# Second mlp in two halves of its width, with blocks in pairs

## Chip, cores and metric

The kernel runs on one core of one Trainium2 chip. The metric is the device time of one execution in microseconds (us), as the median of several runs; less is better.

## The reference, cut to what matters

Three layers follow each other on 4 x 768 = 3072 tokens of 384 values: a linear attention with a decaying state (8 heads of 48), a soft mixture of experts (8 experts of 4 slots, width 1024), and a second mlp of width 2048. All is float32.

```python
def _attn_ref(r, k, v, w, u):
    for t in range(S):
        cur = np.einsum('bhd,bhe->bhde', u[None] * kt, vt)
        y[:, :, t] = np.einsum('bhd,bhde->bhe', rt, state + cur)
        state = w[None, :, :, None] * state + np.einsum('bhd,bhe->bhde', kt, vt)
def _moe_ref(x, phi, w1, w2):
    logits = x @ phi
    # d: softmax over the tokens, c: softmax over the 32 slots
    slot_input = d.T @ x
    for e in range(E):
        h = np.maximum(slot_input[e] @ w1[e], 0.0)
        slot_out[e] = h @ w2[e]
    return c @ slot_out
def _moe2_ref(x, w_in, w_out):
    h = x @ w_in
    g = np.maximum(0.01 * h, h)
    return g @ w_out
```

The inputs w_in and w_out of the second mlp come as float64 and have to be brought to float32 on the chip; all other inputs are float32.

## The kernel before, in words

One function, `chunked`, writes the work out by hand (its order on each engine is the order of the code). It has three parts.

*The attention* goes over 24 units `i`, one for each of 6 chunks of 128 tokens and 4 pairs of heads. Each unit loads its rows `rkb` and its tokens `tk` from HBM four units ahead; GpSimd scales and multiplies them (lines 300, 306, 309, 338), VectorE scales the other half (300), masks the scores (`copy_predicated`, 357), sums a diagonal (314) and adds to the state (410); TensorE computes scores, outputs and updates (349, 380, 387, 400). Every fourth unit adds a softmax over the slots (lines 457 to 509). Beside it the weights of the later parts are loaded: `WST` says at which unit the next tile is loaded by `load_weights`, first 8 tiles `wir` of w_in (128 x 768 values of 8 bytes, as pairs of integers), then the 16 tiles of w1. They lie in the pool `wp`, a ring of `NWT` = 16 buffers of 6 KiB per partition. The tiles of w_in are brought to float32 in half tiles, one in each of the units of `NARROW` (4 to 19): `narrow_a` on ScalarE into PSUM (`nra`, line 166), and `narrow_b`, `narrow_c` and `narrow_d` on VectorE (lines 170, 174, 180), whose result goes to `wi` in SBUF.

*The experts* are TensorE's: `hidden` (line 718) and `outer` (line 761), with the last rows of w2 (`load_rows`) and all eight tiles `wor` of w_out (`load_wout`) loaded meanwhile into buffers of the ring that come free.

*The second mlp* never forms the tokens' x. The 32 slots' outputs are multiplied with w_in once, G = slot_out x w_in (`pG`, line 849: 32 x 2048, in two halves of columns `x`, four column groups `j` of 512 side by side in the partitions). G is split in a rounded value and its rest (`gch`, `gcl`), and `spread` (lines 868, 869) brings each group back to a layout of 128 rows, `Gs`. Then 96 steps `n` follow, one for each of 6 blocks of 512 tokens and 16 tiles `f` of 128 columns of the width, block by block (`seq`, line 874). A step has a hidden matmul (`hid_a`: `h` in PSUM, line 893, and its scaling by 0.01 on ScalarE, line 897), the maximum on VectorE (`hid_b`, line 900, into `t`), a rounded copy on ScalarE (`hid_c`, line 903, `gh`) and the rest that the rounding lost (`hid_d`, line 907, `gl`; on GpSimd in the first 16 steps, on VectorE later). `product` (line 946) adds nine matmuls to the three output tiles of the block: gh x woh, gh x wol and gl x woh, where woh and wol are w_out rounded and its rest. The hidden matmul runs three steps ahead of its product, the cast and the rest two steps ahead:

```python
        if n + 2 < n_seq:
            hid_c(n + 2)
        if n + 3 < n_seq:
            hid_a(n + 3)
```

PSUM holds two tiles of `h` (pool `pH`) and two sets of three output tiles (pool `pP`): eight tiles of 128 x 512 together. Within the first 12 steps a chunk `p` of w_out is narrowed every second step: `conv_a` on ScalarE (line 806, the abs of the high word, into `wfa` in SBUF), `conv_b`, `conv_c`, `conv_d` on VectorE (again lines 170, 174, 180, whole tiles of 768 columns). `parts(f)` then makes woh on ScalarE (line 821) and wol on GpSimd (line 822), one tile f per step. At the end of a block `store` copies its three tiles to SBUF (line 953) and SP stores them; the last three tiles f of the last block are done output tile by output tile.

Of the kernel before, what the change touches and what calls it, by code (L numbers as in the profile page):

```python
# [115 lines left out]
def chunked(ctx, tc, rk, tok, wT, urep, phi, w1, w2, win, wout, outT, dbg=None, check=False):  # L116
# [655 lines left out]

    def load_rows(f):
        t = wp.tile([128, 4, DM], F32, name=f"w2_{f}", tag="wt")
        nc.sync.dma_start(t, w2[4:, :, f].rearrange("e p d -> p e d"))
        for g in range(4):
            w2_sb[FT * (4 + g) + f] = t[:, g]
# [64 lines left out]
    gch = ep.tile([128, 512], F32R, name="gch", tag="hs", bufs=2)  # L842
    gcl = ep.tile([128, 512], F32R, name="gcl", tag="hs", bufs=2)
    for x in range(2):
        k = slice(x * 256, x * 256 + 256)
        pG = pE.tile([128, 256], F32, name=f"pG{x}", tag="ph")
# [7 lines left out]
        nc.scalar.copy(gch[:, k], pG)
        nc.vector.tensor_tensor(gcl[:, k], pG, gch[:, k].bitcast(F32), op=ALU.subtract)
        if x == 0:
            parts(0)
            conv_b(1)
        else:
            conv_c(1)  # L860


    def spread(j, xs, pool, tag):
        pg = pool.tile([128, 2, 256], F32, name=f"pg{j}{xs[0]}", tag=tag)
        hi, lo = (sel[:, j, z : z + 4].rearrange("p a s -> p (a s)") for z in (1, 0))
        for n, x in enumerate(xs):
            k = slice(x * 256, x * 256 + 256)
            nc.tensor.matmul(pg[:, n], hi, gch[:, k], start=True, stop=False)
# [200 lines left out]
```

## Time and profile before

| what | us |
|---|---|
| median of 3 runs | 419.74 |
| lowest and highest run | 418.54, 421.74 |
| the profiled execution, whole | 415.55 |
| its span (first to last instruction) | 413.8 |
| TensorE busy in the span | 384.6 |
| VectorE busy | 291.5 |
| ScalarE busy | 236.7 |
| GpSimd busy | 153.1 |

The profile is of one execution, a little faster than the median. Times in its rows count from the start of the span. An engine's busy time is the time in which one of its instructions ran; what an engine waited for before an instruction stands behind the bar in the view by groups of lines, and in brackets in the timeline. A matmul of float32 operands shows as two instructions in the trace (48 for the 24 of `pG`). Numbers at the end of a line name in the view by stretch: TensorE's granted clock as a share of full speed, the share of time in which the DMA engines were busy, and GB/s.

### The profile page before, as it was taken

What the parts mean: (1) busy time and instruction counts of PE and PEld (TensorE: products, weight loads), DVE (VectorE), ACT (ScalarE), POOL (GpSimd) and SP (SyncE); (2) the same over time, 40 slices, a digit from 0 to 9 for tenths busy, and PEclk for the clock granted to TensorE, in tenths of its full rate; (3) what the DMA queues carried; (4) which work ended last, traced back from release to release, by engine and by line L of the source; (5) the groups of instructions that cost most, each with busy time, mean ns of one, the idle gap of its engine ahead of it and who ended that gap; (6) DMA issues with size and microseconds to landing.
All of it is one profiled execution on the core that took longest, in us unless ns stands there. A gap on an engine that the chain in (4) does not pass through costs nothing.

```text
span 413.8 us, 7910 instructions
## 1 busy us (share of the span) xinstructions
PE 384.6 (93%) x2929; PEld 289.6 (70%) x2929; DVE 291.5 (70%) x496; ACT 236.7 (57%) x544; POOL 153.1 (37%) x142
## 2 busy tenths in 40 slices
PE   5798998989999999988889999999999999999993
PEld 3477786868676444666568888888888888888882
DVE  6988999999994642898866666665656575665650
ACT  4577777777786402686665554645555555555440
POOL 4989997978770400299992000000000000000000
PEclk9979999999999999999999999999999999999998
DMA  7969999999999899910002000200200020001002
GB/s 257 408 246 389 410 399 408 397 408 389 407 360 326 267 358 389 417 54 0 1 2 77 0 2 0 76 2 1 78 0 0 2 77 0 2 36 40 2 0 84
DMA packets 20944, 70.06 MB, mean 169 GB/s; under 512 B 2225, under 2 KB 7073, under 8 KB 20769
## 3 DMA queue, kind: packets, MB, share of 16 engines
q1 hardware_dynamic: 20896, 69.47, 43.9%
q8 instruction: 25, 0.41, 0.4%
q14 instruction: 23, 0.18, 0.2%
HBM read 64.74 MB, written 4.72 MB: 168 GB/s over the span
## 4 chain that ended last, share of the span: by engine, by line
PE 60%; DVE 22%; ACT 5%; POOL 4%; issue 4%; DMA 2%; SPq 1%; DVEq 0%; ACTq 0%; POOLq 0%
PE o L946 43%; DVE base L357 5%; PE h L893 5%; ACT base L329 3%; PE po L761 3%; PE ph L718 3%; DVE wor L174 2%; DVE Sbd L410 2%; DVE rkb L300 2%; DVE Dg L314 2%; POOL gl L907 2%; DVE nra L174 2%; DMA rkb<-in_rk_dram 2%; PE A L349 1%; DVE wor L170 1%
## 5 line engine op out<-in xcount | busy, mean ns | idle before, releaser
L903 ACT CAST gh<-t 128x512 fp32r<-128x512 f32 x94 | 58.4, 621 | 70.6 <-DVE t L900 67.5
L907 DVE TENSOR_TENSOR gl<-t,gh 128x512 fp32r<-128x512 f32 x80 | 55.4, 692 | 58.7 <-ACT gh L903 56.9
L946 PE MATMUL o<-gl,woh 128*128 128x512 f32 x282 | 82.1, 396 | 0.7 <-POOL gl L907 0.7
L946 PE MATMUL o<-gh,wol 128*128 128x512 f32 x282 | 82.2, 396 | 0.0
L946 PE MATMUL o<-gh,woh 128*128 128x512 f32 x282 | 81.4, 393 | 0.0
L900 DVE TENSOR_TENSOR t<-t,h 128x512 f32<-128x512 f32 x96 | 65.7, 685 | 16.4 <-ACT t L897 16.0
L897 ACT ACTIVATE t<-h 128x512 f32<-128x512 f32 x96 | 57.3, 598 | 23.0 <-PE h L893 16.2
L329 ACT ACTIVATE base<-anti,Dg 128x128 f32<-128x128 f32 x184 | 56.3, 389 | 15.2 <-DVE Dg L314 15.0
L946 PEld LDWEIGHTS o<-gl,woh 128*128 128x128 f32 x282 | 52.9, 188 | 14.2 <-POOL gl L907 1.6
L946 PEld LDWEIGHTS o<-gh,wol 128*128 128x128 f32 x282 | 53.0, 188 | 12.7
L946 PEld LDWEIGHTS o<-gh,woh 128*128 128x128 f32 x282 | 52.9, 188 | 11.6
L893 PE MATMUL h<-cT,Gs 128*128 128x512 f32 x96 | 38.5, 405 | 5.7 <-DVE t L900 5.2
L300 POOL TENSOR_TENSOR rkb<-rkb,ET 112x512 f32<-112x512 f32 x24 | 31.9, 1328 | 11.4 <-DMA rkb<-in_rk_dram 11.4
L349 PE MATMUL A<-rkb 48*128 48x128 f32 x384 | 29.7, 297 | 6.5 <-DVE base L357 3.4
L357 DVE COPY_PREDICATED base<-mask,A 128x512 f32<-128x512 int32 x48 | 32.5, 727 | 2.1 <-PE A L349 1.1
L349 PEld LDWEIGHTS A<-rkb 48*128 48x128 f32 x384 | 25.2, 199 | 11.7 <-POOL tk L309 4.4
L822 POOL TENSOR_TENSOR wol<-wor,woh 128x384 fp32r<-128x384 f32 x16 | 22.1, 1385 | 28.8 <-PE pg L869 28.5
L893 PEld LDWEIGHTS h<-cT,Gs 128*128 128x128 f32 x96 | 18.0, 189 | 14.0 <-DVE t L900 9.5
L387 PE MATMUL y<-base,tk 128*48 128x128 f32 (+1 forms) x376 | 26.4, 284 | 0.0
L306 POOL TENSOR_TENSOR tk<-tk,u_sb 128x384 f32<-128x384 f32 x23 | 24.6, 1068 | 2.2 <-DMA tk<-in_tok_dram 1.1
L309 POOL TENSOR_TENSOR tk<-tk 128x384 f32<-128x384 f32 x23 | 24.1, 1048 | 1.8
L387 PEld LDWEIGHTS y<-base,tk 128*48 128x48 f32 (+1 forms) x376 | 20.2, 127 | 3.9 <-issue 1.0
(181 smaller groups left out, 489.8 us busy)
## 6 DMA issues: line engine op xcount, KB each, us to landing
w<-in_w_dram SPq DMA_DIRECT2D x24, 768.0 KB, 8.6
tk<-in_tok_dram SPq DMA_DIRECT2D x23, 576.0 KB, 7.1
rkb<-in_rk_dram SPq DMA_DIRECT2D x24, 512.0 KB, 7.3
wir<-in_win_dram SPq DMA_DIRECT2D x8, 768.0 KB, 9.0
wor<-in_wout_dram SPq DMA_DIRECT2D x8, 768.0 KB, 14.5
out_dram<-obs SPq DMA_DIRECT2D x18, 256.0 KB, 2.3
w2t<-in_w_dram SPq DMA_DIRECT2D x4, 576.0 KB, 5.9
rkb<-in_w_dram SPq DMA_DIRECT2D x4, 384.0 KB, 7.0
```

The source lines that it names most:

```text
L300: (nc.vector if x else eng).tensor_tensor(t, t, e, op=ALU.mult)
L306: eng.tensor_tensor(rr, rr, u_sb[:, hp : hp + 1, :].broadcast_to([128, B, 2 * D]), op=ALU.mult)
L329: nc.scalar.activation(base[i][:, h, b, :], anti, AF.Copy, scale=Dg[i][:, h * B + b : h * B + b + 1])
L349: nc.tensor.matmul(a[:, h, b, :], rk_t[i][p0 : p0 + D, 1, b, :], rk_t[i][p0 : p0 + D, 0, b, :], start=True, stop=True,)
L357: nc.vector.copy_predicated(base[i][:, :, 2 * j : 2 * j + 2, :], mask.unsqueeze(1).unsqueeze(1).broadcast_to([128, 2, 2, C]), a[:, :, 2 * ...
L387: nc.tensor.matmul(y[64 * h : 64 * h + n, b, :], v[:, b, D * h : D * h + n], base[i][:, h, b, :], start=c == 0, stop=True, skip_group_chec ...
L893: nc.tensor.matmul(h, Gs[f // 8][:, f % 8 * 128 : f % 8 * 128 + 128], cT[blk // 3][:, blk % 3 * TB : blk % 3 * TB + TB], start=True, stop= ...
L897: nc.scalar.mul(tt[n], h, 0.01)
L900: nc.vector.tensor_tensor(tt[n], tt[n], hps[n], op=ALU.max)
L903: nc.scalar.copy(gh[n], tt[n])
L907: eng.tensor_tensor(gl[n], tt[n], gh[n].bitcast(F32), op=ALU.subtract)
L946: nc.tensor.matmul(os[m], w[j][:, k, m * 128 : (m + 1) * 128], g[n], start=f == 0 and w is woh and g is gh, stop=f == NFT - 1 and g is gl,)
```

## The change

The width of the second mlp is done in two halves of eight tiles f, and within a half the six blocks go in three pairs: for each tile f the two blocks of the pair follow each other, so that a tile of w_out serves two steps in a row (`seq`). Only the last two blocks of the second half go one after the other. After the first half of a block its three output tiles are copied to SBUF (`sums`, six tiles of the ring); after the second half `store` adds the PSUM tiles to them on VectorE and stores the sum.

What only the second half needs is done within the first. Four of the eight tiles of w_in (0 to 3, columns of the first half) are loaded and narrowed in the attention, in eight units instead of sixteen; the other four are loaded after the experts and narrowed whole at steps 14, 18, 22 and 26 (in SBUF, as w_out is). Their buffers then take the tiles 4 to 7 of w_out (`again`), which are narrowed at steps 34, 38, 42 and 46. A table `jobs` says what is done in which step. The second half of G is computed at step 30 in a PSUM tile of `h`, and spread at steps 32 and 33. GpSimd makes `gl` for odd steps of the first half, VectorE for all others. `WST` has 22 tiles instead of 24: four of w_in, sixteen of w1, two rows of w2; the ring has 18 buffers instead of 16. `conv_b` of chunk 1 stands in the code ahead of the steps and again at step 0.

The core of the diff (with new functions in full; left out are the renamed layout of w_in, tiles that change their pool, and the debugging output):

```diff
-NWT = 16
+NWT = 18
...
-WST = [2, 3, 4, 5, 5, 6, 7, 8, 9, 9, 10, 11, 12, 13, 13, 14, 15, 16, 17, 17, 18, 19, 20, 21]
-NARROW = list(range(4, 20))
+WST = [2, 3, 4, 5, 6, 7, 8, 8, 9, 10, 11, 12, 12, 13, 14, 15, 16, 17, 19, 20, 21, 22]
+NARROW = [5, 7, 9, 11, 12, 14, 16, 18]
 WCH = 8
+WH = WCH // 2
...
+    for j in range(WH, WCH):
+        wirs[j] = wp.tile([128, WCW, 2], I32, name=f"wir{j}", tag="wt")
+        load_wide(win[j], wirs[j])
...
+    def g_mm(x, pool, tag):
+        pG = pGs[x] = pool.tile([128, 256], F32, name=f"pG{x}", tag=tag)
         for kt in range(KT):
             for j in range(4):
                 nc.tensor.matmul(
                     pG[32 * j : 32 * j + 32, :], soT[:, kt, :],
...
+                    wi[:, j, kt * 256 : kt * 256 + 256], start=kt == 0, stop=kt == KT - 1,
...
+    def g_parts(x, pool, tag):
...
+        nc.scalar.copy(gch[x], pGs[x])
+        nc.vector.tensor_tensor(gcl[x], pGs[x], gch[x].bitcast(F32), op=ALU.subtract)
...
+    g_mm(0, pE, "ph")
+    g_parts(0, ep, "hs")
+    parts(0)
+    conv_b(1)
...
-    seq = [(blk, f) for blk in range(NTOK // TB) for f in range(NFT)]
+    seq = [
+        (blk, f) for x in range(2) for two in range(0, NB, 2)
+        for f in range(NFT // 2 * x, NFT // 2 * (x + 1)) for blk in (two, two + 1)
+    ]
+
+    seq[-NFT:] = sorted(seq[-NFT:])
...
-        eng = nc.gpsimd if 0 < n < NFT else nc.vector
+        eng = nc.gpsimd if 0 < n < n_seq // 2 and n % 2 else nc.vector
...
     hid_c(1)
-    conv_d(1)
+    parts(1)
     hid_d(1)
     late[1](nc.scalar.copy)
-    late[2](nc.vector.tensor_copy)
-    late[3](nc.scalar.copy)
+    conv_a(1)
...
     def store(blk, m, o):
-        ob = obs[blk % 2][:, m, :]
-        (nc.scalar.copy if m % 2 else nc.vector.tensor_copy)(ob, o)
-        nc.sync.dma_start(outT[m * 128 : (m + 1) * 128, blk * TB : (blk + 1) * TB], ob)
+        t = sums[blk][:, m, :]
+        nc.vector.tensor_tensor(t, t, o, op=ALU.add)
+        nc.sync.dma_start(outT[m * 128 : (m + 1) * 128, blk * TB : (blk + 1) * TB], t)
...
+    def convert(p, n):
+        if p > 1:
+            job(n - 2, conv_a, p)
+        job(n, conv_b, p)
+        job(n, conv_c, p)
+        job(n + 1, conv_d, p)
+        if p < WCH:
+            job(n + 2, parts, 2 * p)
+            job(n + 3, parts, 2 * p + 1)
+
+    for p in range(1, WH):
+        convert(p, 4 * (p - 1))
+    def again(p):
+        wor[p] = wirs[p]
+        load_wide(wout[p], wor[p])
+
+    for q in range(WH):
+        convert(WCH + q, 4 * q + 14)
+        job(4 * q + 18, again, WH + q)
+        convert(WH + q, 4 * q + 34)
+    late = {}
+    job(30, g_mm, 1, pH, "h")
+    job(31, g_parts, 1, gp, "g1")
+    for q in range(2):
+        job(32 + q, lambda q: late.update({q: spread(1, (2 * q, 2 * q + 1), pH, "h")}), q)
+        job(32 + q, lambda q: late[q](nc.scalar.copy), q)
...
+        for fn, a in jobs.get(n, ()):
+            fn(*a)
         if not last:
             product(n, range(KT), pout[blk])
+        if f == NFT // 2 - 1:
+            for m in range(KT):
+                (nc.vector.tensor_copy if m % 2 else nc.scalar.copy)(
+                    sums[blk][:, m, :], pout[blk][m]
+                )
```

Chunks `p` of 8 and above are the tiles of w_in: `raw(p)` is `wor[p]` below 8 and `wirs[p - 4]` from there, and `conv_d` of those writes `wi[:, p - 8]`.

What moves on the engines shows at three places. First VectorE in the attention: one unit and the beginning of the next, before:

```order
L300 TENSOR_TENSOR rkb_111<-rkb_111,ETp 112x512
L357 COPY_PREDICATED base_998<-mask,A_1041 128x2x256 x2
L314 TENSOR_REDUCE Dg_1069<-tk_871 128x4x2
L410 SCALAR_TENSOR_TENSOR Sbd<-Sbd,W_138,U_1081 48x4x48 x2
L170 TENSOR_SCALAR wir_557<-wir_557 128x384
L174 SCALAR_TENSOR_TENSOR nra_1032<-nra_1032,wir_557 128x384
L180 SCALAR_TENSOR_TENSOR wi<-wir_557,nra_1032 128x384
L300 TENSOR_TENSOR rkb_112<-rkb_112,ETp 112x512
```

and after the change, at the unit with the same buffer `rkb_111`:

```order
L300 TENSOR_TENSOR rkb_111<-rkb_111,ETp 112x512
L357 COPY_PREDICATED base_981<-mask,A_1022 128x2x256 x2
L314 TENSOR_REDUCE Dg_1050<-tk_859 128x4x2
L410 SCALAR_TENSOR_TENSOR Sbd<-Sbd,W_138,U_1062 48x4x48 x2
L300 TENSOR_TENSOR rkb_112<-rkb_112,ETp 112x512
```

The three instructions of the narrowing are gone from this unit; the unit ahead of it keeps its own.

Second, VectorE at the start of the second mlp, before (the number behind `t`, `g`, `h` and `gl` is the step, that behind `wor` the chunk of w_out):

```order
L855 TENSOR_TENSOR gcl_2338<-pG0_2339,gch_2337 128x256
L170 TENSOR_SCALAR wor1_2165<-wor1_2165 128x768
L855 TENSOR_TENSOR gcl_2338<-pG1_2357,gch_2337 128x256
L174 SCALAR_TENSOR_TENSOR wor1_2165<-wfa_2277,wor1_2165 128x768
L900 TENSOR_TENSOR t0_2382<-t0_2382,h0_2381 128x512
L900 TENSOR_TENSOR t1_2387<-t1_2387,h1_2386 128x512
L907 TENSOR_TENSOR g0_2383<-t0_2382,g0_2383 128x512
L180 SCALAR_TENSOR_TENSOR wor1_2165<-wor1_2165 128x768
L871 CAST Gs1_2172<-pg20_2399 128x512
L900 TENSOR_TENSOR t2_2436<-t2_2436,h2_2435 128x512
L170 TENSOR_SCALAR wor2_2167<-wor2_2167 128x768
L174 SCALAR_TENSOR_TENSOR wor2_2167<-wfa_2277,wor2_2167 128x768
```

and after:

```order
L876 TENSOR_TENSOR gcl0_2311<-pG0_2297,gch0_2310 128x256
L170 TENSOR_SCALAR wor1_2071<-wor1_2071 128x768
L925 TENSOR_TENSOR t0_2322<-t0_2322,h0_2321 128x512
L925 TENSOR_TENSOR t1_2326<-t1_2326,h1_2325 128x512
L932 TENSOR_TENSOR g0_2125<-t0_2322,g0_2125 128x512
L925 TENSOR_TENSOR t2_2364<-t2_2364,h2_2363 128x512
L932 TENSOR_TENSOR gl2_2366<-t2_2364,gh2_2365 128x512
L925 TENSOR_TENSOR t3_2375<-t3_2375,h3_2374 128x512
L170 TENSOR_SCALAR wor1_2071<-wor1_2071 128x768
L174 SCALAR_TENSOR_TENSOR wor1_2071<-wfa_2223,wor1_2071 128x768
L925 TENSOR_TENSOR t4_2398<-t4_2398,h4_2397 128x512
L180 SCALAR_TENSOR_TENSOR wor1_2071<-wor1_2071 128x768
```

The maxima t0 to t3 now stand ahead of the second and third part of chunk 1's narrowing, `gl2` and `gl4` are VectorE's, and chunk 2 does not come in these rows any more.

Third, TensorE at G, before (`pG0` and `pG1` are the two halves of G, `pg` are spreads):

```order
L849 MATMUL pG0_2339<-wi_74,soT_2332 32x256 x12
L849 MATMUL pG1_2357<-wi_74,soT_2332 32x256 x12
L868 MATMUL pg00_2375<-gch_2337,sel_2054 128x256
L869 MATMUL pg00_2375<-gcl_2338,sel_2054 128x256
L893 MATMUL h0_2381<-cT0_2161,Gs0_2171 128x512
L893 MATMUL h1_2386<-cT0_2161,Gs0_2171 128x512
L868 MATMUL pg01_2391<-gch_2337,sel_2054 128x256
L869 MATMUL pg01_2391<-gcl_2338,sel_2054 128x256
```

and the second half of G after the change, at step 30 (`o2_0` to `o2_2` are the output tiles of block 2, `h33` and `h34` hidden matmuls of steps 33 and 34):

```order
L918 MATMUL h33_2971<-cT1_2122,Gs0_2123 128x512
L867 MATMUL pG1_2980<-wi_74,soT_2292 32x256 x12
L967 MATMUL o2_0_0_2697<-gh30_2918,woh0_2220 128x512
L967 MATMUL o2_1_0_2698<-gh30_2918,woh0_2220 128x512
L967 MATMUL o2_2_0_2699<-gh30_2918,woh0_2220 128x512
L967 MATMUL o2_0_0_2697<-gh30_2918,wol0_2222 128x512
L967 MATMUL o2_1_0_2698<-gh30_2918,wol0_2222 128x512
L967 MATMUL o2_2_0_2699<-gh30_2918,wol0_2222 128x512
L967 MATMUL o2_0_0_2697<-gl30_2919,woh0_2220 128x512
L967 MATMUL o2_1_0_2698<-gl30_2919,woh0_2220 128x512
L967 MATMUL o2_2_0_2699<-gl30_2919,woh0_2220 128x512
L918 MATMUL h34_3006<-cT1_2122,Gs0_2123 128x512
```

The twelve matmuls of `pG1` went from the wait before step 0 to between the hidden matmul of step 33 and the product of step 30.

## Rows read from the trace of the kernel before

**Rows 1.** view by stretch, four stages; columns are named in its first line

```profile
core 0: us, PE busy (x) PEld busy (x) DVE busy (x) ACT busy (x) POOL busy (x), PEclk, DMA share, GB/s
45.00:124.20 79.20, 73.89 (x1062) 59.56 (x1062) 75.82 (x155) 60.46 (x186) 66.17 (x63) 1.00 1.00 397
...
138.80:166.40 27.60, 27.33 (x270) 11.41 (x270) 12.01 (x28) 5.06 (x14) 4.40 (x10) 1.00 0.99 349
...
175.16:212.06 36.90, 30.98 (x122) 21.77 (x121) 32.85 (x33) 24.84 (x45) 35.37 (x23) 1.00 0.06 23
212.06:406.80 194.74, 194.71 (x837) 156.79 (x835) 117.69 (x174) 102.63 (x173) 7.58 (x7) 1.00 0.06 24
```

**Rows 2.** the chain that ended last, from the page, by line

```profile
PE o L946 43%; DVE base L357 5%; PE h L893 5%; ACT base L329 3%; PE po L761 3%; PE ph L718 3%; DVE wor L174 2%; DVE Sbd L410 2%; DVE rkb L300 2%; DVE Dg L314 2%; POOL gl L907 2%; DVE nra L174 2%; DMA rkb<-in_rk_dram 2%; PE A L349 1%; DVE wor L170 1%
```

**Rows 3.** groups of lines between 45 and 124.2 us

```profile
L300 POOL TENSOR_TENSOR rkb<-rkb,ET 112x512 f32<-112x512 f32 x15 | 19.4, 1295 | 6.1 <-DMA rkb<-in_rk_dram 6.1
...
L174 DVE SCALAR_TENSOR_TENSOR nra<-nra,wir 128x384 int32<-128x384 int32 x16 | 9.1, 567 | 2.0 <-ACT base L329 0.5
L180 DVE SCALAR_TENSOR_TENSOR wi<-wir,nra 128x384 int32<-128x384 int32 x16 | 8.9, 554 | 0.5
...
L170 DVE TENSOR_SCALAR wir<-wir 128x384 int32<-128x384 uint32 x16 | 7.6, 473 | 0.3
```

**Rows 4.** TensorE's timeline, steps 0, 1, 2, 12 and 13 of the second mlp

```profile
175.16 0.95 PE L946 MATMUL o<-g,woh 128*128 128x512 f32 x3
...
178.26 0.86 PE L946 MATMUL o<-g,woh 128*128 128x512 f32 x3
...
182.19 0.86 PE L946 MATMUL o<-gh,woh 128*128 128x512 f32 x3
...
212.06 0.87 PE L946 MATMUL o<-gh,woh 128*128 128x512 f32 x3
...
214.38 0.86 PE L946 MATMUL o<-gh,woh 128*128 128x512 f32 x3
```

**Rows 5.** groups of lines between 175.16 and 212.06 us

```profile
L907 POOL TENSOR_TENSOR gl<-t,gh 128x512 fp32r<-128x512 f32 x11 | 18.7, 1696 | 0.7 <-ACT gh L903 0.7
L822 POOL TENSOR_TENSOR wol<-wor,woh 128x384 fp32r<-128x384 f32 x11 | 15.6, 1415 | 0.3 <-ACT woh L821 0.3
L174 DVE SCALAR_TENSOR_TENSOR wor<-wfa,wor 128x768 int32<-128x768 int32 x6 | 10.8, 1792 | 0.3
...
L180 DVE SCALAR_TENSOR_TENSOR wor<-wor 128x768 int32<-128x768 int32 x7 | 8.8, 1256 | 0.0
...
L170 DVE TENSOR_SCALAR wor<-wor 128x768 int32<-128x768 uint32 x6 | 6.6, 1104 | 0.0
L821 ACT CAST woh<-wor 128x384 fp32r<-128x384 f32 x12 | 6.5, 540 | 0.4 <-DVE wor L180 0.4
...
L806 ACT ACTIVATE wfa<-wor 128x768 f32<-128x768 f32 x6 | 5.4, 905 | 0.0
```

**Rows 6.** ScalarE's timeline at the first steps

```profile
174.46 1.22 ACT L903 CAST g<-t 128x512 fp32r<-128x512 f32 x2
...
176.54 0.61 ACT L897 ACTIVATE t<-h 128x512 f32<-128x512 f32 x1
```

**Rows 7.** TensorE's timeline: G, and the first and last late spread

```profile
168.74 2.80 PE L849 MATMUL pG<-wi,soT 128*32 128x256 f32 x48 [0.35 <-DVE soT L837]
...
173.03 0.28 PE L868 MATMUL pg<-gch,sel 128*128 128x256 f32 x1
...
174.57 0.28 PE L869 MATMUL pg<-gcl,sel 128*128 128x256 f32 x1
```

**Rows 8.** groups of lines between 212.06 and 400 us

```profile
L900 DVE TENSOR_TENSOR t<-t,h 128x512 f32<-128x512 f32 x82 | 56.3, 686 | 12.6 <-ACT t L897 12.4
L907 DVE TENSOR_TENSOR gl<-t,gh 128x512 fp32r<-128x512 f32 x79 | 54.7, 692 | 57.9 <-ACT gh L903 56.1 <-PE h L893 1.5
...
L953 DVE COPY obs<-o 128x512 f32<-128x512 f32 x10 | 6.4, 686 | 1.0 <-PE o L946 1.0
```

More of the change, by code (lines that the diff above doesn't have):

```diff
@@ L770, in load_wout, with block_sums @@
         load_wide(wout[j], wor[j])
[L773 to L777, printed above, removed]
     hs0 = hidden(0)
-    for f in range(FT):
+    for f in range(2, FT):
         load_rows(f)
+    for j in range(2):
+        load_wout(j)
     mix(0)
     hs1 = hidden(1, lambda: hidden_t(0, hs0))
+    for j in range(2, WH):
+        load_wout(j)
     cT = [wp.tile([128, NTOK // 2], F32R, name=f"cT{x}", tag="wt") for x in range(2)]
     cT4 = [t.rearrange("p (b n t) -> p b n t", b=B // 2, n=NC) for t in cT]
-    for j in range(4):
-        load_wout(j)
     Gs = [wp.tile([128, FF // 2], F32R, name=f"Gs{x}", tag="wt") for x in range(2)]
+    g01 = [wp.tile([128, 2, TB], F32R, name=f"g{n}", tag="wt") for n in range(2)]
+    sums = {}
+    def block_sums(blk):
+        sums[blk] = wp.tile([128, KT, TB], F32, name=f"sum{blk}", tag="wt")
     mix(1)
@@ L840, in chunked @@
     conv_d(0)
[L842 to L846, printed above, removed]
+    gch, gcl, pGs = {}, {}, {}
+    def g_mm(x, pool, tag):
+        pG = pGs[x] = pool.tile([128, 256], F32, name=f"pG{x}", tag=tag)
         for kt in range(KT):
@@ L850, in chunked @@
                     pG[32 * j : 32 * j + 32, :], soT[:, kt, :],
-                    wi[:, j, kt * 512 + x * 256 : kt * 512 + x * 256 + 256],
-                    start=kt == 0, stop=kt == KT - 1,
-                )
[L854 to L868, printed above, removed]
-            nc.tensor.matmul(pg[:, n], lo, gcl[:, k], start=False, stop=True)
-        out = Gs[j // 2][:, j % 2 * 512 + xs[0] * 256 : j % 2 * 512 + xs[-1] * 256 + 256]
-        return lambda copy: copy(out.rearrange("p (x t) -> p x t", t=256), pg[:, 0 : len(xs)])
@@ L874, in chunked, with spread @@
-    seq = [(blk, f) for blk in range(NTOK // TB) for f in range(NFT)]
+                    wi[:, j, kt * 256 : kt * 256 + 256], start=kt == 0, stop=kt == KT - 1,
+                )
+    def g_parts(x, pool, tag):
+        gch[x] = pool.tile([128, 256], F32R, name=f"gch{x}", tag=tag, bufs=2)
+        gcl[x] = pool.tile([128, 256], F32R, name=f"gcl{x}", tag=tag, bufs=2)
+        nc.scalar.copy(gch[x], pGs[x])
+        nc.vector.tensor_tensor(gcl[x], pGs[x], gch[x].bitcast(F32), op=ALU.subtract)
+    def spread(x, js, pool, tag):
+        pg = pool.tile([128, 2, 256], F32, name=f"pg{x}{js[0]}", tag=tag)
+        for n, j in enumerate(js):
+            hi, lo = (sel[:, j, z : z + 4].rearrange("p a s -> p (a s)") for z in (1, 0))
+            nc.tensor.matmul(pg[:, n], hi, gch[x], start=True, stop=False)
+            nc.tensor.matmul(pg[:, n], lo, gcl[x], start=False, stop=True)
+        out = Gs[x][:, js[0] * 256 : js[-1] * 256 + 256]
+        return lambda copy: copy(out.rearrange("p (x t) -> p x t", t=256), pg[:, 0 : len(js)])
@@ L884, in hid_a @@
             tt[n] = ep.tile([128, TB], F32, name=f"t{n}", tag="cst", bufs=2)
-            g = wp.tile([128, 2, TB], F32R, name=f"g{n}", tag="wt")
-            gh[n], gl[n] = g[:, 0], g[:, 1]
+            gh[n], gl[n] = (g01[n][:, x] for x in range(2))
         else:
```

72 lines of the change are left out of this document (36 added, 36 removed).

## The prediction

> **What bounds the kernel now.** I read the view by stretch first [rows 1]. The reader is to see four stages with different limits. From 45 to 124.2 us, the units of the attention, VectorE is busy 75.82 of 79.20 us, TensorE 73.89, GpSimd 66.17, and the DMA engines all the time at 397 GB/s. From 138.8 to 166.4 TensorE is busy 27.33 of 27.60: the experts, which the change leaves alone. From 175.16 to 212.06 TensorE does 30.98 of 36.90 while GpSimd is busy 35.37 and VectorE 32.85: the first twelve steps of the second mlp, beside which the weights of its output are narrowed and split. From 212.06 on TensorE is busy 194.71 of 194.74 and nothing else counts. The chain that ended last agrees [rows 2]: TensorE's products hold 43% of it, and the rest is cut among VectorE's lines of the attention (357, 410, 300, 314, 174, 170), the experts' matmuls and the narrowing. So time can come out of the attention's units and of the twelve slow steps; after that every microsecond put on TensorE is a microsecond of the kernel.
>
> **The change, part 1: half of the narrowing leaves the attention.** A half chunk costs VectorE 0.473 + 0.567 + 0.554 = 1.594 us (lines 170, 174, 180 [rows 3]); eight of sixteen go: 12.8 us. VectorE is the bound there, but the others stand close behind. TensorE idles 79.20 - 73.89 = 5.3 us in the stretch, and all its work stays. The DMA engines moved 79.2 us x 397 GB/s = 31.4 MB; SP's order has 21 weight tiles of 786 kB ahead of the last unit's load, and 18 after the change, so 2.36 MB less, 5.9 us at that rate. GpSimd waited 6.1 us for loads of rkb [rows 3], which says that the loads are at their limit already. The gain lies between 0 (loads keep the pace, the eight units that still narrow keep theirs) and 5.3 us. I take 3.5, two thirds of TensorE's idle time: TensorE at 100% is seen only in the second mlp, where each step is alike. What is late next is TensorE with the loads. The rows of w2 that move ahead of the experts (two of eight) and the other reordered loads cost nothing: TensorE bounds the experts, and by then fewer bytes are queued than before.
>
> **Part 2: the start of the second mlp.** Before, step 0 begins at 175.16 and step 12 at 212.06, 36.90 us for twelve steps that later take 214.38 - 212.06 = 2.32 each [rows 4]: 27.8, so 9.1 us are lost. GpSimd does one gl (1.696) and one wol (1.415) in each, 3.11 us, more than a step; VectorE does a narrowing of 1.104 + 1.792 + 1.256 = 4.15 us every two steps [rows 5]. Now two blocks share each tile of the width, so one chunk lasts four steps. Per four steps (9.3 us): GpSimd two gl and two wol, 6.2; VectorE four t (0.686), two gl (0.692) [rows 8] and one narrowing, 8.3 even at its slow durations; ScalarE four times the scaling (0.61) and the cast (half of 1.22) [rows 6], one abs (0.905) and two casts (0.540), 6.9. All fit, and TensorE works two to three steps behind them.
>
> The first steps I follow by hand. VectorE's queue puts t0 and t1 ahead of the second narrowing now, but t0 still waits for h0, so step 0 begins about where it did, 175.1. ScalarE gets more ahead of the scaling of t2: the two casts of g end at 174.46 + 1.22 = 175.7, then a weight cast (0.54), one copy of Gs (half of the 0.86 left between 175.68 and 176.54 for two) and the abs of chunk 1 (0.905) run to 177.5, where before the scaling began at 176.54 [rows 6]. The scaling (0.61) and the maximum (0.686) free the bank of h for step 1 at 178.8; with its own hidden matmul (ten such make a step of 2.32, with its fill I take 0.3) the product of step 1 begins at 179.05, against 178.26 before. Step 2 follows at 181.4 (before: 182.19), and nothing after it is late: step 12 at 181.4 + 10 x 2.32 = 204.6, against 212.06. That is 7.4 us gained. The upper bound is the whole loss, 9.1; the lower one half of it, 4.5, if the slow durations of lines 170 and 174 still stall TensorE. That conv_b of chunk 1 is issued twice adds 0.6 to 1.1 us on VectorE, inside this.
>
> What speaks against the change here is where the moved narrowing reads. In the attention the first operand of line 174 lies in PSUM and 384 columns take 0.567 us, so 768 would take 1.13; in the second mlp both operands lie in SBUF, beside a busy GpSimd, and 768 take 1.792 [rows 3, 5]. The Trainium skill says in SBUF — State Buffer, section Who interferes with whom, that a VectorE instruction with two SBUF inputs contends with a GpSimd instruction that reads SBUF, and that the second to start is blocked until the first ends. The trace agrees, 1.792 against 1.13. For the four chunks of w_in that move it makes 4.15 instead of 2 x 1.594 = 3.19 us each, some 4 us more of VectorE, at steps 14 to 27. VectorE is idle there: 57.9 us of idle time stand before gl in the even stretch [rows 8]. The same holds for the output's chunks 4 to 7, now at steps 34 to 47. I cost both at nothing; the cover would be gone only if a narrowing lasted over two steps, and it lasts 4.15 of 4.64.
>
> **Part 3: the second half of G.** Its 24 matmuls (half of 2.80 us) and four spreads of two matmuls each go from the wait before step 0, where VectorE set the pace, to steps 30 to 33, where TensorE does. The fourteen late matmuls of the spreads run from 173.03 to 174.57 + 0.12, 0.12 each [rows 7]. So 1.40 + 8 x 0.12 = 2.4 us are added to TensorE. G takes one of the two banks of h: the hidden matmul of step 32 needs gch and gcl read, ScalarE's cast for them stands behind two copies of block 2's sums (some 0.6 to 0.7 each), and I add 0.7 for that. Together 3.1; bounds 2.4 and 6, one step and a half more, if the four tiles in two banks stall each of four steps.
>
> **Part 4: pairs, sums and stores.** Six sum copies fall to VectorE and twelve to ScalarE, and eighteen additions replace eighteen copies of the same size (0.686 [rows 8]). VectorE does 117.69 of 194.74 us there [rows 1], so the work is hidden. What is new is the exchange: a pair holds all six output banks, so the next pair's first product has to wait until the first block's banks are emptied, and has one step (2.32) for it. In the second half three additions take 2.1 us, the next t and gl 1.4, the second block's three again 2.1: its last bank is free 5.5 us after the first block ended, and asked for after 2 x 2.32 + 0.3 + 0.5 = 5.4. So a tenth or two at each of five exchanges, 0.8 us in all; bounds 0 and 5 (half a step each).
>
> **The sum.** The profiled execution took 415.55 us, 413.8 of them span. -3.5 - 7.4 + 3.1 + 0.8 = -7.0: 408.6 on its scale. The median of the three runs is 419.74, 4.2 above it; the same -7.0 gives 412.7, which I forecast.
>
> **Rivals.**
> - The attention gives nothing (loads or the chain of units keep their pace). For it: DMA share 1.00 and GpSimd's waits. Against it: SP's order really has 2.36 MB less ahead of the last unit. Then -3.5, 416.2. Chance 0.12.
> - The start gives only half, because GpSimd and VectorE go on blocking each other. For it: line 174's 1.792. Against it: half as many GpSimd instructions per step. Then -7.0 + 7.4 - 4.5 = -4.1, 415.6. This is what the rule of the Trainium skill quoted above would bring if every moved narrowing met a GpSimd instruction. Chance 0.13.
> - More than forecast: the attention gives all 5.3, the start 8, the exchanges nothing: -5.3 - 8 + 2.4 = -10.9, 408.8. For it: TensorE's idle time is all that stands in the way. Chance 0.17.
> - Slower: the exchange of banks decides. Place: first product of each pair. If a bank's copy or addition stands behind a narrowing (4.15) and the t and gl of a step, the wait is a step and more; at 3 us for each of five exchanges, 15 us, the result is -7.8 + 15 = +7, 427. It decides from 1.6 us per exchange on (7.8 / 5). For it: steps 14 and 46 carry both a narrowing and a copy. Against it: the narrowing's first two parts end before the product that the copy waits for. Chance 0.04.
>
> **How the numbers follow.** My forecast has 0.54, with its own range 410 to 415.5. Within 1% of 419.74 begins above 415.5; 1% is about what a measurement of this kernel tells from no change. Faster by over 1%: nearly all of the forecast (0.51), the larger gain (0.17), and a little under half of the first two rivals (0.10), 0.78. Slower by over 1%: the last rival, 0.04. The rest, 0.18, is within 1%. The range from 407 to 418 holds the larger gain and both small ones, and leaves out the exchange.
>
> **What would show it right or wrong.** In the changed profile: the stretch from first to last unit shorter by 3 to 4 us, VectorE's share in it down to some 80%; step 12 of the second mlp 29 to 30 us after step 0; the product of step 1 some 4 us after step 0; 24 matmuls of pG1 between two even steps, and a wait of h under 1 us two steps later; no wait of TensorE over 0.5 us at steps 16, 32, 48 and 64. It is wrong if the units take as long as before, if steps 2 to 12 last longer than 2.4 us, or if TensorE waits for a sum's copy or addition at every exchange.

## The result and the profile after

The changed kernel takes 408.12 us (median of 4 runs, 407.27 to 408.63) against 420.14 for the kernel before beside it: a ratio of 0.9712 with a 95% interval from 0.967 to 0.9753, some 12 us less, where 7.0 was forecast. The time lies in the predicted range of 407 to 418, but below the forecast of 412.7 and below the forecast's own 410 to 415.5; nearest is the third rival, the larger gain (408.8, chance 0.17). Executions more than 1.5% above the fastest of their kernel count in the medians and are left out of every ratio.

The profiled execution took 408.15 us (span 406.3). The view by stretch of the changed kernel has three stages here: the units of the attention from the start of the ninth to the start of the last (both at VectorE's line 300), steps 0 to 11 of the second mlp, and the steps after them.

```profile
core 0: us, PE busy (x) PEld busy (x) DVE busy (x) ACT busy (x) POOL busy (x), PEclk, DMA share, GB/s
48.88:120.53 71.65, 70.27 (x1048) 57.62 (x1048) 65.31 (x130) 55.70 (x173) 61.34 (x58) 1.00 1.00 398
...
172.65:202.18 29.53, 28.37 (x121) 22.53 (x122) 21.41 (x29) 20.58 (x37) 16.37 (x13) 1.00 0.00 1
202.18:400.00 197.82, 197.58 (x869) 158.02 (x867) 131.96 (x196) 112.56 (x194) 34.60 (x27) 1.00 0.11 39
```

The units are TensorE's now: it is busy 70.27 us of 71.65, and VectorE 65.31 (91%, where it had 96% of its stretch in [rows 1]). The twelve first steps take 29.53 us instead of 36.90, and GpSimd's work beside them fell from 35.37 us to 16.37. The chain that ended last says the same in one line by engine, first before, then after:

```profile
PE 60%; DVE 22%; ACT 5%; POOL 4%; issue 4%; DMA 2%; SPq 1%; DVEq 0%; ACTq 0%; POOLq 0%
```

```profile
PE 78%; DVE 9%; ACT 6%; DMA 3%; issue 2%; SPq 1%; DVEq 0%; ACTq 0%
```

TensorE's timeline at steps 0, 1, 2 and 12 (start, duration, the wait before in brackets) answers to [rows 4]:

```profile
172.65 0.96 PE L967 MATMUL o<-g,woh 128*128 128x512 f32 x3
...
176.18 0.50 PE L918 MATMUL h<-cT,Gs 128*128 128x512 f32 x1 [1.16 <-DVE t L925]
176.52 0.85 PE L967 MATMUL o<-g,woh 128*128 128x512 f32 x3
...
178.84 0.86 PE L967 MATMUL o<-gh,woh 128*128 128x512 f32 x3
...
202.18 0.86 PE L967 MATMUL o<-gh,woh 128*128 128x512 f32 x3
```

Step 1 comes 3.87 us after step 0 (before: 3.10) and step 2 another 2.32 later (before: 3.93); from there every step takes 2.33. The groups of instructions beside it, between 172.65 and 202.18 us, answer to [rows 5]:

```profile
L932 POOL TENSOR_TENSOR gl<-t,gh 128x512 fp32r<-128x512 f32 x6 | 9.4, 1568 | 7.7 <-ACT gh L928 4.7 <-issue 2.9
...
L836 POOL TENSOR_TENSOR wol<-wor,woh 128x384 fp32r<-128x384 f32 x6 | 6.2, 1038 | 7.5 <-ACT woh L835 7.5
...
L174 DVE SCALAR_TENSOR_TENSOR wor<-wfa,wor 128x768 int32<-128x768 int32 x3 | 2.9, 961 | 0.1
```

GpSimd runs six of each instead of eleven, with 15 us of idle time between them. The second half of G shows in the chain of the changed kernel:

```profile
242.00 2.10 PE o L967 x9
244.10 0.23 PE h L918
244.33 1.43 PE pG L867 x24
245.76 2.07 PE o L967 x8
...
247.85 0.70 DVE sum L1032
...
248.58 0.63 ACT gh L928
249.21 0.51 ACT t L922
...
249.75 0.70 DVE t L925
...
250.49 0.49 PE h L918
...
251.63 2.10 PE o L967 x9
...
254.42 2.09 PE o L967 x9
...
256.74 2.10 PE o L967 x9
```

From 242.00 to 256.74 pass 14.74 us for five steps that would take 11.67 at 2.33 each, so 3.07 more. The view of waits for TensorE's matmuls between 172 and 400 us has every exchange of banks in its stretch (engine and line, what it waited for, us in total, times, longest):

```profile
PE h L918 <- DVE t L925: 1.4, 2, 1.2
```

Both waits lie at the start (1.16 us before step 1, 0.23 before step 0). In this view none stands at an exchange of banks.

So from one profiled execution to the other the sum came out near the forecast, 415.55 to 408.15 or −7.4. Its parts did not: the experts begin 2.4 us earlier (140.5 and 138.2, rows below), where 3.5 was forecast of the attention, and what follows takes 5.0 less, where the forecast of parts 2 to 4 was 3.5. And the medians are 12 us apart; that difference needs another place.

### The profile page after: what moved, and what is told of

It reads as the page before. It is cut to its first block, busy times and chain, and to the rows that moved or that the text cites. A ratio compares the mean times of both kernels' runs of the same rounds, so it can differ in the third digit from the quotient of the medians.

```text
span 406.3 us, 7904 instructions
## 1 busy us (share of the span) xinstructions
PE 381.5 (94%) x2929; PEld 289.9 (71%) x2929; DVE 285.9 (70%) x487; ACT 237.8 (59%) x548; POOL 158.0 (39%) x151
## 4 chain that ended last, share of the span: by engine, by line
PE 78%; DVE 9%; ACT 6%; DMA 3%; issue 2%; SPq 1%; DVEq 0%; ACTq 0%
PE o L967 48%; PE h L918 5%; PE A L349 4%; PE y L380 4%; ACT base L329 4%; PE y L387 3%; DMA rkb<-in_rk_dram 3%; PE po L770 3%; PE ph L727 3%; DVE base L357 2%; PE px L435 2%; PE l L427 1%; PE U L400 1%; PE pS L496 1%; DVE Dg L314 1%
## 5 line engine op out<-in xcount | busy, mean ns | idle before, releaser
L932 DVE TENSOR_TENSOR gl<-t,gh 128x512 fp32r<-128x512 f32 x71 | 50.2, 706 | 40.9 <-ACT gh L928 39.7
L932 POOL TENSOR_TENSOR gl<-t,gh 128x512 fp32r<-128x512 f32 x23 | 34.5, 1498 | 52.3 <-ACT gh L928 49.4
L349 PE MATMUL A<-rkb 48*128 48x128 f32 x384 | 28.8, 291 | 8.0 <-DVE base L357 4.4
L349 PEld LDWEIGHTS A<-rkb 48*128 48x128 f32 x384 | 24.3, 193 | 13.2 <-POOL rkb L300 6.0
L306 POOL TENSOR_TENSOR tk<-tk,u_sb 128x384 f32<-128x384 f32 x23 | 23.6, 1027 | 4.0 <-PE U L400 1.6
L420 ACT COPY xT<-y 112x512 f32<-112x512 f32 x23 | 13.5, 585 | 17.1 <-PE y L387 17.0
L918 PEld LDWEIGHTS h<-cT,Gs 128*128 128x128 f32 x96 | 17.9, 188 | 7.6 <-DVE t L925 2.7
## 6 DMA issues: line engine op xcount, KB each, us to landing
wir<-in_win_dram SPq DMA_DIRECT2D x8, 768.0 KB, 11.8
```

The source lines that it names most:

```text
L349: nc.tensor.matmul(a[:, h, b, :], rk_t[i][p0 : p0 + D, 1, b, :], rk_t[i][p0 : p0 + D, 0, b, :], start=True, stop=True,)
L918: nc.tensor.matmul(h, Gs[f // 8][:, f % 8 * 128 : f % 8 * 128 + 128], cT[blk // 3][:, blk % 3 * TB : blk % 3 * TB + TB], start=True, stop= ...
L932: eng.tensor_tensor(gl[n], tt[n], gh[n].bitcast(F32), op=ALU.subtract)
```

## The experiments

The first theory: parts 2 to 4 are as forecast, and the attention gives twice what I gave it, because the profiled execution of before was a quick one. The rival: the halves of the change help each other, or the second mlp gives more than its trace shows. A second question follows if the attention it is: the narrowing on VectorE, or the 3.1 MB of loads.

**Each part alone.** Four runs: the kernel before once more (e1); before with half of the narrowing and loads in the attention (e2); the changed kernel with its attention as before (e3); and the changed kernel once more (e4). The attention alone (e2), as an edit of the kernel before, leaves out half of w_in:

```diff
-WST = [2, 3, 4, 5, 5, 6, 7, 8, 9, 9, 10, 11, 12, 13, 13, 14, 15, 16, 17, 17, 18, 19, 20, 21]
-NARROW = list(range(4, 20))
+WST = [2, 3, 4, 5, 6, 7, 8, 8, 9, 10, 11, 12, 12, 13, 14, 15, 16, 17, 19, 20]
+NARROW = [5, 7, 9, 11, 12, 14, 16, 18]
...
-        if n < WCH:
+        if n < WCH // 2:
...
-    wi[:, j, kt * 512 + x * 256 : kt * 512 + x * 256 + 256],
+    wi[:, j % 2, kt * 512 + x * 256 : kt * 512 + x * 256 + 256],
```

The second mlp alone (e3), as an edit of the changed kernel; the eight tiles of w_in are loaded and narrowed in the attention again:

```diff
-NWT = 18
+NWT = 16
-WST = [2, 3, 4, 5, 6, 7, 8, 8, 9, 10, 11, 12, 12, 13, 14, 15, 16, 17, 19, 20, 21, 22]
-NARROW = [5, 7, 9, 11, 12, 14, 16, 18]
+WST = [2, 3, 4, 5, 5, 6, 7, 8, 9, 9, 10, 11, 12, 13, 13, 14, 15, 16, 17, 17, 18, 19, 20, 21]
+NARROW = list(range(4, 20))
...
-        convert(WCH + q, 4 * q + 14)
-        job(4 * q + 18, again, WH + q)
...
```

> The kernel before, unchanged, run and profiled again. Theory A (a lowered TensorE clock in the first units of the attention costs some executions 4 to 5 us, the profiled execution of before was one of those that lost least): the runs lie at 418 to 422, the new profile shows a stretch between 20 and 50 us with a granted clock near 0.5 that is longer than the 5 us of the first profile, and its units after 50 us take as long as in the first one. Theory B (the runs are 4 us slower than the profile for another reason, all over the kernel): the stretches after 50 us are longer too. Theory C (the profile was typical): about 415.5.

> Before, with the attention's part of the change alone: four of the eight tiles of w_in are loaded and narrowed (eight half tiles instead of sixteen); the other half of w_in is left out, and G is computed from the first half twice. If TensorE is the next bound in the units (idle 5.3 us in 45 to 124.2): 4 to 5.5 us faster than before, units of 4.4 to 4.8 us, TensorE busy over 97% in them. If the loads keep the pace: under 2 us. If VectorE's 12.8 us count whole: over 8 us.

> After, with the attention's part undone: all eight tiles of w_in are loaded and narrowed in the attention as before (ring of 16 buffers), the second mlp runs in two halves and pairs, with the second half of G at step 30. If the parts add up as forecast (start 7.4 gained, G 3.1 and exchanges 0 to 0.8 lost): 3.5 to 4.5 us faster than before. If the measured 12 us come mainly from the second mlp: 7 us or more faster. If they come mainly from the attention: under 2.

> The kernel after, unchanged, run and profiled again: 407 to 409. Theory A: its new profile shows a low clock between 20 and 50 us again, of other length and place; theory C: the same as in its first profile to a few tenths of a us.

Beside a median of 419.69 us for the kernel before, before again took 421.08 (ratio 1.0034, 0.9989 to 1.0078), the attention alone 411.07 (0.9806, 0.9732 to 0.9881), the second mlp alone 414.25 (0.9911, 0.9863 to 0.9959) and the change again 407.35 (0.9712, 0.9619 to 0.9805). By the ratios the attention gives 8.1 us and the second mlp 3.7, together 11.8 of 12.1: the halves add up, and within these intervals neither needs the other. The second mlp's interval, 1.7 to 5.7, holds its forecast. The attention's, 5.0 to 11.2, leaves out its forecast of 3.5, but by itself it does not rule out the 5.3 us of TensorE's idle time.

The trace of e1 bears out half of its theory A. The granted clock from 20 to 30 us is 0.52, where the first profile had 0.71, and the ninth unit starts 2.3 us later (49.83 against 47.50). But the units after it take 82.79 us instead of 76.72, which A had denied. Theory B is refuted for the second mlp: what follows the attention takes 275.0 us in both (table below).

**Narrowing or loads.** Both kernels start from the kernel before, each with one half of what e2 did. Eight tiles loaded, eight half narrowings (e5):

```diff
-NARROW = list(range(4, 20))
+NARROW = [5, 7, 9, 11, 12, 14, 16, 18]
...
-    wi[:, j, kt * 512 + x * 256 : kt * 512 + x * 256 + 256],
+    wi[:, j % 2, kt * 512 + x * 256 : kt * 512 + x * 256 + 256],
```

Four tiles loaded, sixteen half narrowings, each tile narrowed twice (e6):

```diff
-WST = [2, 3, 4, 5, 5, 6, 7, 8, 9, 9, 10, 11, 12, 13, 13, 14, 15, 16, 17, 17, 18, 19, 20, 21]
+WST = [2, 3, 4, 5, 6, 7, 8, 8, 9, 10, 11, 12, 12, 13, 14, 15, 16, 17, 19, 20]
-        if n < WCH:
+        if n < WCH // 2:
...
-            narrow_b(wirs[j], w)
+            narrow_b(wirs[j // 2], w)
...
```

> The kernel before with all eight tiles of w_in still loaded, but only eight of the sixteen half narrowings done (four tiles are loaded and never narrowed; the second half of G is computed from the first half of w_in, so the output's second half of the width is left wrong in value, with the same amount of matmul work). VectorE loses 8 x 1.594 = 12.8 us in the attention, the loads lose nothing. If VectorE's work sets the pace of the units: units from #9 to the last in 71 to 72.5 us, as in the executions with eight half narrowings and half the loads (71.0 to 71.75), and 6 to 9 us under the kernel before. If the loads set it: units of 76 us and more, under 2 us of gain. In between, 3 to 5 us, both share it.

> The kernel before with only four tiles of w_in loaded (twenty weight tiles in the attention instead of twenty-four) and all sixteen half narrowings done, each tile being narrowed twice (the other four tiles are left out, so the second half of the width is computed from the first half's weights). VectorE's work stays, 3.1 MB of loads go. If VectorE's work sets the pace: units from #9 to the last still take 76 to 83 us and the time is within 2 us of the kernel before. If the loads set it: units of 73 us or less and 6 us or more of gain.

Half of the narrowing takes 409.93 us against 419.4 (ratio 0.9794, 0.9703 to 0.9886); half of the loads 418.22 (0.9964, 0.992 to 1.0008). The views by stretch follow, from the ninth unit to the last, first of half the narrowing and then of half the loads (columns as above):

```profile
44.63:115.76 71.13, 70.31 (x1043) 57.34 (x1041) 65.07 (x131) 54.82 (x171) 60.90 (x57) 1.00 1.02 412
```

```profile
46.09:126.64 80.55, 72.07 (x1037) 57.21 (x1035) 77.35 (x152) 58.54 (x180) 63.61 (x60) 1.00 0.90 343
```

With half the narrowing TensorE fills the stretch (70.31 of 71.13) while the DMA engines run all the time at 412 GB/s; e2, with half of the loads gone as well, takes 71.02, no less. With half the loads they are down to 0.90 and 343 GB/s, and the units take 80.55 us all the same, VectorE busy 77.35 of them. TensorE waits for this in the two stretches, in the same order (total, times, longest; of the second view the three longest):

```profile
PE px L435 <- DVE Sbd L410: 0.3, 1, 0.3
PE pt L486 <- ACT d L467: 0.3, 1, 0.3
PE A L349 <- PE px L435: 0.2, 1, 0.2
```

```profile
PE px L435 <- DVE Sbd L410: 3.5, 3, 1.5
PE A L349 <- DMA w<-in_w_dram: 1.4, 3, 0.6
PE A L349 <- DVE base L357: 1.2, 2, 0.6
...
```

The narrowing decides, and the bytes hardly count (1.5 us by the ratio, whose interval goes from 3.4 us to no gain). That it is VectorE's part of the narrowing is argued: e5 also leaves out eight `narrow_a` on ScalarE, and what points at VectorE are its 77.35 us of 80.55 and the 4.7 us of waits for it, against 0.8 for ScalarE. The second view also puts 1.4 us down to loads of w1, in the kernel with fewer loads; that is not explained. The DMA share of 1.00 that I held against part 1 says that a transfer is always under way, not that anything waits for it.

**Where the executions differ.** The first matmul of the experts (`ph`) closes the attention. Its rows follow (minimum, median and maximum in ns, then first and last start), from before, before again, half the loads, the second mlp alone, half the narrowing, the change, and the change again:

```profile
L718 PEld LDWEIGHTS ph<-w,slT x96: 105/110/110, 140.5 to 151.2; 128*32 128x32 f32 x96
```

```profile
L718 PEld LDWEIGHTS ph<-w,slT x96: 105/110/110, 148.9 to 159.6; 128*32 128x32 f32 x96
```

```profile
L718 PEld LDWEIGHTS ph<-w,slT x96: 105/110/110, 142.9 to 153.6; 128*32 128x32 f32 x96
```

```profile
L725 PEld LDWEIGHTS ph<-w,slT x96: 106/110/110, 147.7 to 158.4; 128*32 128x32 f32 x96
```

```profile
L718 PEld LDWEIGHTS ph<-w,slT x96: 105/110/110, 133.6 to 144.2; 128*32 128x32 f32 x96
```

```profile
L727 PEld LDWEIGHTS ph<-w,slT x96: 105/110/110, 138.2 to 148.8; 128*32 128x32 f32 x96
```

```profile
L727 PEld LDWEIGHTS ph<-w,slT x96: 106/110/111, 136.5 to 147.1; 128*32 128x32 f32 x96
```

Taken from the time of the same execution, the first start splits it (all columns in us):

| profiled execution | whole | experts begin | what follows | ninth to last unit |
|---|---|---|---|---|
| before | 415.55 | 140.5 | 275.0 | 76.7 |
| before again | 423.92 | 148.9 | 275.0 | 82.8 |
| half the loads | 417.72 | 142.9 | 274.8 | 80.55 |
| half the narrowing | 408.04 | 133.6 | 274.4 | 71.13 |
| attention alone | 408.47 | 134.0 | 274.5 | 71.02 |
| second mlp alone | 418.0 | 147.7 | 270.3 | 80.25 |
| the change | 408.15 | 138.2 | 270.0 | 71.65 |
| the change again | 406.61 | 136.5 | 270.1 | 71.75 |

What follows the attention agrees within 0.6 us over the old second mlp and within 0.4 over the new one, where it is 4.6 less on the mean. Nearly all the spread between executions is in the attention. With sixteen half narrowings the long run of units takes 76.7 to 82.8 us in four executions; with eight, 70.5 to 72.8 in nine (the later runs included). The profiled execution of before had the shortest of the long ones. What makes the long ones differ by 6 us no run shows.

Not all of the shorter run arrives: from the last unit's start on VectorE to the experts pass 16.3 us with sixteen half narrowings and 17.3 to 17.9 with eight, some 1.4 more. Units of 80.5 us that become 71.5 so give 7.6. The result gives the same from the other side: 12.1 us by its ratio less the 4.6 of what follows leaves 7.5 for the attention (5.8 to 9.3 by the interval), more than the 5.3.

**An earlier or a later start of the loads.** In the changed kernel the ninth unit starts at 48.88 us, in e5 at 44.63. Two stretches of the change between 30 and 40 us:

```profile
30.00:35.00 5.00, 2.69 (x52) 2.06 (x48) 4.96 (x10) 2.96 (x10) 4.92 (x6) 1.00 0.93 352
35.00:40.00 5.00, 4.26 (x28) 3.81 (x30) 4.77 (x10) 3.14 (x10) 4.84 (x5) 0.53 0.75 301
```

TensorE is idle for almost half of the first five microseconds; then its granted clock is 0.53, near the lower of its two levels (1.2 of 2.4 GHz), and 28 matmuls run where 52 ran before. Two tables of load times try to prevent it, first the early one, then the late one:

```diff
-WST = [2, 3, 4, 5, 6, 7, 8, 8, 9, 10, 11, 12, 12, 13, 14, 15, 16, 17, 19, 20, 21, 22]
+WST = [1, 2, 4, 5, 6, 7, 8, 8, 9, 10, 11, 12, 12, 13, 14, 15, 16, 17, 19, 20, 21, 22]
```

```diff
-WST = [2, 3, 4, 5, 6, 7, 8, 8, 9, 10, 11, 12, 12, 13, 14, 15, 16, 17, 19, 20, 21, 22]
-NARROW = [5, 7, 9, 11, 12, 14, 16, 18]
+WST = [4, 5, 6, 6, 7, 8, 9, 9, 10, 11, 12, 13, 13, 14, 15, 16, 17, 18, 19, 20, 21, 22]
+NARROW = [7, 9, 10, 11, 13, 14, 16, 18]
```

> The changed kernel with its first two weight loads one unit earlier (units 1 and 2 instead of 2 and 3) and none at unit 3, so that they fall into the 20 to 25 us of the span in which the DMA engines were idle, ahead of the rkb loads that GpSimd waited for. If the early wait for rkb (6.45 us in the profiled execution) and the fall of the granted clock behind it (0.53 at 35 to 40 us) come from weight tiles queued ahead of rkb: 1 to 3 us less than the changed kernel, 404 to 406. If they come from the total of bytes that are under way: no difference, 406 to 409.

> The changed kernel with its weight loads begun at unit 4 instead of 2 and the eight half narrowings from unit 7 on, so that the first units' own rows are loaded alone. If weight tiles ahead of rkb make the early wait and the clock's fall: 2 to 4 us less than the changed kernel, 403 to 406, with a granted clock of 0.9 and over from 30 us on. If the same bytes only cost the same later (w1 late for the experts or rkb late at units 10 to 18): no difference or up to 3 us more, 407 to 411.

> The changed kernel as it is, beside the next two on the same chip: 404 to 409 us (so far 408.12 and 407.35), units from #9 to the last in 71 to 72.5 us.

> The changed kernel with its first two weight loads one unit earlier, once more with more rounds. If the early wait for rkb and the fall of the clock behind it are from weight tiles queued ahead of rkb: again 1 to 3 us under the changed kernel beside it. If 405.96 was chance: within 1 us of it.

The early table took 405.96 us (ratio to before 0.9686, 0.9585 to 0.9787) and, in a second try with more executions, 406.36 (0.9675, 0.9649 to 0.9701); the change beside the second 407.4 (0.9677, 0.9631 to 0.9723). The late table took 407.24 (0.9717, 0.962 to 0.9813). The medians of the early table are the lowest in both tries, by about 1 us, and its second interval lies within that of the change beside it: not shown to be better. Nor do the traces bear the theory out. The late table has a granted clock of 1.00 from 30 us on, as its theory wanted, and gains nothing. In the first early execution the ninth unit starts at 44.62 us; in the second the clock falls all the same, only sooner:

```profile
15.00:20.00 5.00, 2.31 (x36) 1.46 (x34) 4.93 (x8) 4.37 (x16) 4.92 (x5) 1.00 1.03 412
20.00:25.00 5.00, 5.00 (x49) 4.25 (x49) 4.71 (x11) 3.39 (x12) 4.12 (x5) 0.50 0.86 347
25.00:30.00 5.00, 5.00 (x47) 4.02 (x45) 2.58 (x5) 2.40 (x8) 4.01 (x4) 0.50 0.77 281
```

Ahead of this fall too TensorE had been idle for part of the time (2.31 of 5 us busy). Why it falls in some executions and at different places stays open.

**Was GpSimd relieved by the pairs or by VectorE?** The change halves GpSimd's `wol` per step through the pairs, and hands every second `gl` to VectorE. The last run (e11) undoes the second part.

```diff
-        eng = nc.gpsimd if 0 < n < n_seq // 2 and n % 2 else nc.vector
+        eng = nc.gpsimd if 0 < n < n_seq // 2 else nc.vector
```

> The changed kernel with all rests gl of the first half's steps on GpSimd (in the changed kernel the odd ones only, VectorE the even ones). If the pairs alone take GpSimd out of the way (half as many wol per step): four gl at 1.5 to 1.7 and two wol at 1.0 to 1.4 make 8.0 to 9.6 us per four steps of 9.3, so TensorE waits for gl at few steps and the time is 0 to 2 us more than the changed kernel's. If the other half of the gain at the start came from taking every second gl off GpSimd: a step as long as GpSimd's share while it also slows the narrowing, 2.5 us and more for 12 to 24 steps, 3 to 8 us more.

It takes 407.76 us against 407.4 for the change beside it (ratio 0.9671, 0.9627 to 0.9716, to before): no difference. These are its groups between 170 and 270 us, and all waits of TensorE's matmuls between 172 and 400:

```profile
L932 POOL TENSOR_TENSOR gl<-t,gh 128x512 fp32r<-128x512 f32 x40 | 57.0, 1424 | 29.9 <-ACT gh L928 27.5 <-PE o L967 1.4 <-PE pg L884 1.0
...
L836 POOL TENSOR_TENSOR wol<-wor,woh 128x384 fp32r<-128x384 f32 x8 | 8.3, 1032 | 31.6 <-ACT woh L835 31.6
...
L174 DVE SCALAR_TENSOR_TENSOR wor<-wfa,wor 128x768 int32<-128x768 int32 x3 | 4.9, 1626 | 0.1
```

```profile
PE h L918 <- DVE t L925: 0.2, 1, 0.2
```

Four `gl` and two `wol` are 4 x 1.42 + 2 x 1.03 = 7.8 us per four steps of 9.3: the pairs alone are enough. Line 174 is slow again here, 1.626 us on the mean, and TensorE doesn't notice. The pairs halve two things per step, GpSimd's `wol` and VectorE's narrowing, and the maxima `t1` to `t3` moved ahead of a narrowing as well; which of these did it no run separates.

## Why the prediction was right, and where it was off

- **Part 2, the start of the second mlp, −7.4.** The steps 0 to 12 came from 36.90 us down to 29.53: −7.4. Put on the axis of before by the distance of the experts' starts (2.36), step 1 began at 178.9, step 2 at 181.2 and step 12 at 204.5, against 179.05, 181.4 and 204.6 by hand. That the maximum makes step 1 late is the 1.16 us in the row. The pairs alone are enough for the gain, as e11 shows.
- **Part 3, the second half of G, +3.1.** It is 3.07 in the chain, and of the kind I named. The matmuls of G take 1.43; from 250.98 to 251.63 and from 253.95 to 254.42 the spreads take 1.12; the rest, some 0.5, is the bank of `h` (0.7 by the forecast). The matmul at 250.49 waits for the maximum `t` at 249.75, which stands behind the copies of block 2's sums from 247.85 on; I had put G's own cast in that place.
- **Part 4, exchanges, +0.8.** They cost nothing beyond the 0.5 of part 3, which falls at one of them: the view of waits has two, both at the start. My own figures had stood a tenth apart (free after 5.5 us, asked for after 5.4), and I rounded that up to "a tenth or two". The rival that ended slower needs 1.6 us per exchange and has none.
- **The slow narrowing** did not move along, at line 174. I set 4.15 us for a chunk; between 202 and 300 us the three lines take 0.555 + 0.960 + 1.13 to 1.22, some 2.7 (rows below, the view by groups of lines in that stretch of the changed kernel). GpSimd was not idle there: it was busy 34.60 of these 98 us. What counts is which instruction starts first. In the changed kernel line 174 takes 0.96 us every time; at 178.62 it starts ahead of a `gl`, which then lasts 1.84 us, where a `gl` by itself takes 1.30, and line 180 starts within that `gl` and takes 1.46 instead of 0.96 (second rows below). In e11 two of the three in the first steps start within a `gl` and take 1.93 and 1.99, the third starts ahead of one and takes 0.96. So the cost did not go away: it moved to line 180 and to GpSimd, and TensorE does not wait for either. This agrees with what the Trainium skill says in SBUF — State Buffer, section Who interferes with whom: a VectorE instruction with two SBUF inputs contends with a GpSimd instruction that reads SBUF, and the order in which they start decides which one blocks. My comparison with 1.13 was too high as well: in the trace of before, line 174 took 0.96 us at 169.25, where GpSimd stood still.

```profile
L174 DVE SCALAR_TENSOR_TENSOR wir<-wfa,wir 128x768 int32<-128x768 int32 x8 | 7.7, 960 | 0.3
...
L180 DVE SCALAR_TENSOR_TENSOR wi<-wir 128x768 int32<-128x768 int32 x4 | 4.9, 1223 | 0.0
L180 DVE SCALAR_TENSOR_TENSOR wir<-wir 128x768 int32<-128x768 int32 x4 | 4.5, 1133 | 0.0
L170 DVE TENSOR_SCALAR wir<-wir 128x768 int32<-128x768 uint32 x8 | 4.4, 555 | 0.0
```

```profile
178.62 0.96 DVE L174 SCALAR_TENSOR_TENSOR wor<-wfa,wor 128x768 int32<-128x768 int32 x1
...
180.09 1.46 DVE L180 SCALAR_TENSOR_TENSOR wor<-wor 128x768 int32<-128x768 int32 x1
```

```profile
178.90 1.84 POOL L932 TENSOR_TENSOR gl<-t,gh 128x512 fp32r<-128x512 f32 x1 [2.91 <-issue]
```

- Parts 2 to 4 together: −4.6 by the table above, −3.5 by the forecast; 0.8 of the difference is the exchanges, and the last 0.3 is within the 0.6 us by which executions differ there.
- **Part 1, the attention, −3.5: this is the term that failed.** "I take 3.5, two thirds of TensorE's idle time", with the bounds "between 0 (...) and 5.3 us". It is 8.1 by e2's ratio and 7.5 by the result less what follows; e5 gives all of it and e6 next to nothing. Two steps were wrong. First, TensorE does reach its own pace: the two thirds rested on "TensorE at 100% is seen only in the second mlp", and the stretch of e5 shows 70.31 of 71.13. [rows 1] had the experts at 27.33 of 27.60 already. Second, the bound of 5.3 was the idle time of one execution, and the sum was then carried over: "the same -7.0 gives 412.7". With units of 80.55 us (e6) the idle time of TensorE is 80.55 - 72.07 = 8.5 us, and a bound of that size should have stood there. That the 4.2 us between the median of before and its profiled execution lie in these units is inferred: the execution of e6 that has them, 417.72, is near e6's own median of 418.22, but no execution at the median of before was profiled.
- That the profiled pair (−7.4) agrees so well with the forecast (−7.0) is luck. The execution of before was a quick one, while that of the change (408.15) stands at its median (408.12); and within the pair two misses cancel, 2.4 us from the attention instead of 3.5 and 5.0 from what follows instead of 3.5.

## What to carry to other kernels

Before a gain worked out from one profile is put on the median, ask where the executions of the kernel differ: if the spread lies in the stage that the change relieves, the gain on the median can be larger by up to that distance. A DMA share of 1.00, as in e5 and before, says that transfers are under way and no more; whether anything waits for them is a question for a run with fewer loads, as e6 is. And to take a resource out of the way, share what it makes among more steps (a tile for two blocks) before its work is handed to another engine.

## What was not expected of the hardware

TensorE's granted clock falls to about half in single stretches of the attention, near the lower of its two levels (0.53 at 35 to 40 us in the change, 0.50 at 20 to 30 us in the early table's second execution). Of the nine profiled executions with eight half narrowings, the three with a fall at 35 to 40 us (0.52 to 0.54) start the ninth unit at 48.88 to 49.69 us, the other six at 44.62 to 47.40; that the fall makes it late is not shown by a run. In the change it came behind five microseconds with TensorE busy 2.69. Half the loads had 2.84 in the same five and kept 1.00:

```profile
30.00:35.00 5.00, 2.84 (x53) 2.24 (x48) 4.94 (x10) 4.09 (x14) 4.92 (x5) 1.00 0.96 379
35.00:40.00 5.00, 5.00 (x74) 4.36 (x75) 4.85 (x12) 4.65 (x16) 4.84 (x5) 1.00 0.88 327
```

So idle time alone, by these rows, does not tell when it falls.
